# The output product of the last two token groups as seven products of quarters, chained in two PSUM banks

## The chip, the cores and the metric

The kernel runs on one core of a Trainium2 chip. The metric is the device time of one execution in microseconds, as the median of several executions. Before the change it is 307.48 us (three runs, 306.88 to 308.18).

## The reference

Attention over pooled keys and values, followed by a feed-forward layer whose activation is h - tanh(h):

```python
# q, k, v: [8 batches, 8 heads, 576, 64] fp32; pool = 8, Sp = 72
k_p = k.reshape(B, H, Sp, pool, D).mean(axis=3)
v_p = v.reshape(B, H, Sp, pool, D).mean(axis=3)
scores = scale * np.matmul(q, k_p.transpose(0, 1, 3, 2))
attn = softmax(scores)                       # written out in the reference
x = (attn @ v_p) with heads side by side     # [4608 tokens, 512]
h = x @ w_in                                 # w_in  [512, 2048]
g = h - np.tanh(h)
out = g @ w_out                              # w_out [2048, 512], out fp32
```

## The kernel before

The 4608 tokens are worked off in nine groups of 512. Groups 0 to 7 are the first 512 tokens of a batch each; a token 4p + j of the batch is row p of token block j. Group 8 gathers the 64 tokens left over from each of the eight batches; its token block tb holds the rest of batches 2tb and 2tb + 1, 64 rows each.

A group has two matmul stages on TensorE, both in bf16 with fp32 sums in PSUM. The first (`h_mms`, line 386) makes h transposed, in 16 units of 128 of the 2048 hidden features: four matmuls of 512 columns each into one PSUM bank. After every second unit `h_act` lets ScalarE (ACT) take the tanh of two banks into `t_sb` (line 399) and VectorE (DVE) subtract it, which gives two of the 16 slices of `gT` in bf16 (line 400). `gT` is [128 features of a slice, 16 slices, 512 tokens]. The second stage (`o_mms`, line 429) multiplies `gT` with `w2b` ([128, 16 slices, 512 output features], bf16): for each of the four token blocks 16 matmuls of 128 tokens by 512 columns are summed in one bank, so 64 matmuls a group. The list `UNITS` orders them by (token block, quarter of the slices), so that the last slices are asked for late. `o_store` (line 450) copies a finished bank into one of four rotating tiles `o_sb`, and SyncE's queue (SP) stores it: one DMA of 128 rows for groups 0 to 7, two of 64 rows each for group 8. For the very last token block `o_last` splits the columns in 384 and 128, each with its own copy and two stores, one from SP and one from ACT (line 464).

While group g runs, the attention of batch g + 1 is made in between, by the dictionary `plan`: step kinds "s" (scores, lines 275, 287, 290), "e" (exponential, line 303), "t" and "x" (transposes by DMA on SP), "a" (values and normalising, lines 339, 360, 361), at fixed places among the units. Pooling of k and v runs on GpSimd (POOL, lines 193 to 220); loads of q, k and v are issued from SP by `load_for`. Group 6 makes the attention of batch 7 and of the last left-over tokens; groups 7 and 8 hold the two matmul stages alone. The raw tiles `k_raw`, `v_raw` and `q_raw` (two each, fp32, by parity of the batch) are read for the last time in groups 4 and 5 (even batches), and in groups 5 and 6 (batch 7). Each engine works through its own instructions in the order in which the program gives them, since the schedule is manual; TensorE, ACT, DVE, POOL and SP wait for each other only on the data and the buffers.

PSUM has eight banks of 512 fp32 columns. The h units of a group take banks 0 to 5 in turn (`i % 6`); the output product of groups 1 to 8 takes banks 4 and 5 by the parity of the token block, and `o_last` banks 0 and 1.

Of the kernel before, what the change touches and what calls it, by code (L numbers as in the profile page):

```python
# [8 lines left out]
FP32 = mybir.dt.float32  # L9
# [11 lines left out]
R = 4  # L21
# [5 lines left out]
NG = 9  # L27
NT = 5
NK = H * G
KP = 2 * G  # L30
D1 = D + 1
SCALE = 1.0 / (POOL * float(D) ** 0.5)


@with_exitstack
def kernel(
# [13 lines left out]
    const = ctx.enter_context(tc.tile_pool(name="const", bufs=1))  # L50
    work = ctx.enter_context(tc.tile_pool(name="work", bufs=2))
    tpool = ctx.enter_context(tc.tile_pool(name="tpool", bufs=3))
    opool = ctx.enter_context(tc.tile_pool(name="opool", bufs=4))
    psum = ctx.enter_context(tc.tile_pool(name="psum", bufs=1, space=PSUM))
    PS = psum.tile([128, 8, 512], FP32, name="PS")
    ctx.enter_context(tc.manual_schedule())
# [4 lines left out]
    def two(banks, n):  # L61
# [32 lines left out]
    v_sm = const.tile([128, NT, 1, D], FP32, name="v_sm")  # L94
    x_tl = const.tile([128, 1, 2, 4, D], BF16, name="x_tl")
    warm = const.tile([128, 1], FP32, name="warm")
    v_bf = [
        v_raw[i]
        .rearrange("p t n -> p (t n)")
# [1 line left out]
        .rearrange("p (t n) -> p t n", t=NT)  # L101
        for i in range(2)
    ]

    def xT_of(g):
        return xTs[g % 2] if g < B else xTt
# [320 lines left out]
    def o_mms(tb, i0, i1, bank, c0=0, c1=DM):  # L427
        for i in range(i0, i1):
            nc.tensor.matmul(  # L429
                PS[:, bank, 0 : c1 - c0],  # L430
                lhsT=gT[:, i, tb * 128 : (tb + 1) * 128],
                rhs=w2b[:, i, c0:c1],
                start=(i == 0),
                stop=(i == NHID - 1),
            )

    def out_rows(g, tb):
        if g < B:
            blk = out[g * S : g * S + QA, :].rearrange("(p j) m -> p j m", j=R)
            return [(0, 128, blk[:, tb, :])]  # L440
        return [
            (64 * s, 64 * s + 64, out[(2 * tb + s) * S + QA : (2 * tb + s + 1) * S, :])
            for s in range(2)
        ]
# [1 line left out]
    stores = []  # L446

    def o_store(g, tb, bank, eng):
        o_sb = opool.tile([128, DM], FP32, name="o_sb", tag="o_sb")
        eng(out=o_sb[:, :], in_=PS[:, bank, :])  # L450
        for r0, r1, dst in out_rows(g, tb):
            stores.append(
                lambda dst=dst, src=o_sb[r0:r1, :]: nc.sync.dma_start(out=dst, in_=src)
            )

    def o_last(g, tb, banks):
        o_sb = opool.tile([128, DM], FP32, name="o_sb", tag="o_sb")
        for n, (c0, c1, eng) in enumerate(
            ((0, 384, nc.scalar.copy), (384, DM, nc.vector.tensor_copy))
        ):  # L460
            o_mms(tb, 0, NHID, banks[n], c0, c1)
            eng(out=o_sb[:, c0:c1], in_=PS[:, banks[n], 0 : c1 - c0])
            for s, (r0, r1, dst) in enumerate(out_rows(g, tb)):
                (nc.sync, nc.scalar)[s].dma_start(out=dst[:, c0:c1], in_=o_sb[r0:r1, c0:c1])

    def fill(n, bank, cols=512):
        for _ in range(n):
# [234 lines left out]
    PAIRS = ((6, 7), (0, 1), (2, 3))  # L702
    UNITS = [(0, 0), (0, 1), (0, 2), (1, 0), (1, 1), (0, 3), (1, 2), (1, 3)]
    UNITS += [(tb, qd) for tb in (2, 3) for qd in range(4)]
    hn = [0]
    for g in range(1, NG):
        nb = g + 1 if g + 1 < B else None
        more = nb is not None and nb + 1 < B

        tail = {2: 0, 3: 1, 5: 2, 7: 3}.get(nb)  # L710
        plan = {}
        if nb is not None:
            units = [(s_block(nb, j), av_block(nb), slot(4 * nb + j)) for j in range(4)]
            s_pairs, a_pairs = [0, 0, 0, 1, 2], [0, 1, 0, 2, 1]
            plan = {
                -12: [("s", 0)],
                -9: [("e", 0)],
                -8: [("s", 1)],
                -5: [("e", 1), ("t", 0)],
                -3: [("s", 2)],  # L720
                0: [("e", 2)],
                1: [("s", 3)],
                3: [("e", 3), ("t", 1)],
                4: [("a", 0)],
                5: [("a", 1), ("x", 0)],
                9: [("a", 2), ("a", 3), ("x", 1)],
            }
            if g == 1:
                plan[-10], plan[-7], plan[-5] = plan.pop(-12), plan.pop(-9), plan.pop(-8)
                plan[-2], plan[-1] = [("e", 1), ("t", 0)], plan.pop(-3)  # L730
            if tail is not None:
                units.append((s_tail(tail), av_tail(tail), slot_tl))
                plan[3].append(("s", 4))
                plan[4] += [("e", 4), ("t", 2)]
                if g == 1:
                    plan[6], plan[7] = plan[4][:1], plan.pop(5)
                    plan[4] = plan[4][1:]
                    plan[10] = plan.pop(9)
                plan[12] = [("a", 4), ("x", 2)]
            xs = [x_pair(), x_pair(), x_tl]  # L740
        if nb is not None:
            pool_v(nb, nc.gpsimd)
        shs = {}

        def step(kind, n):
            if kind == "t":
                e_turn_dma(units[2 * n][2], 0, 2 if n < 2 else 1)
                if tail and n == 0:
                    turn_tail(tail)
                return  # L750
            if kind == "x":
                x_turn_dma(xs[n], *((nb, 2 * n, 2) if n < 2 else (B, tail, 1)))
                return
            s, a, sl = units[n]
            if kind == "s":
                bk = PAIRS[s_pairs[n]]
                s_mms(s, bk)
                shs[n] = s_shift(bk)
            elif kind == "e":
                s_exp(shs[n], sl)  # L760
            else:
                bk = PAIRS[a_pairs[n]]
                av_mms(sl, a, bk)
                normalise(bk, xs[n // 2][:, n % 2, :, :, :])

        for i in range(NHID):
            h_mms(g, i, i % 6)
            if i % 2:
                h_act(i - 1, (i - 1) % 6)
            for it in plan.get(i - NHID, ()):  # L770
                step(*it)
            if more and i in (13, 15):
                q_cast(nb + 1, se, i - 13, i - 11)
        for u, (tb, qd) in enumerate(UNITS):
            if g == NG - 1 and tb == 3:
                o_last(g, tb, (0, 1))
                break
            o_mms(tb, qd * 4, qd * 4 + 4, 4 + tb % 2)
            if qd == 3:
                o_store(g, tb, 4 + tb % 2, se)  # L780
                run(stores)
            for it in plan.get(u, ()):
                step(*it)
            if u == 0 and more:
                pool_k(nb + 1, nc.gpsimd)
            if more:
                if u == 0:
                    q_turn_dma(nb + 1)
                    run(stores)
                if u == 4:  # L790
                    k_turn_dma(nb + 1)
                    k_place_kT(nb + 1, ge)
                if u == 11 and nb % 2 == 0:
                    run(tail_pieces(nb // 2))
                    tail_cast(nb // 2)
            if u == 13:
                load_for(g + 1)

# [1 line left out]
_INS = ['q', 'k', 'v', 'moe_w_in', 'moe_w_out']  # L800
# [26 lines left out]
```

## Time and profile before

| | |
|---|---|
| median of 3 runs | 307.48 us (306.88 to 308.18) |
| the profiled execution's own time | 306.89 us |
| its span, first to last instruction | 305.10 us |
| mean granted TensorE clock | 0.994 |
| TensorE matmul / weight load busy | 290.4 / 150.4 us |
| DVE / ACT / POOL busy | 179.4 / 142.3 / 113.5 us |
| group 7: first stage, output product | 246.16 to 259.97, 259.97 to 273.79 us |
| group 8: first stage, output product | 273.79 to 287.60, 287.60 to 301.63 us |

In the rows shown below a line has the source line, the engine, the operation, what is written and read, the shapes, and how often it occurs; behind the bar stand the busy time in us and the mean of one in ns, and behind the next bar the idle time of the engine before it and what ended it. In a timeline the first number is the start in us from the span's start and the second is how long the run of instructions takes. Matmul ends are modelled and overlap the next start, so lengths of matmul work are taken from start to start. PEld is the weight load of TensorE; SPq and ACTq are the issuing of DMAs by those engines. The row PEclk gives the granted clock in tenths, for 40 slices of the span.

### The profile page before, as it was taken

The numbers are of one execution on the slowest core, as the hardware profiler recorded it, in microseconds if no ns is written. First come the engines' busy times: TensorE is split into PE (matmuls) and PEld (weight loads), VectorE is DVE, ScalarE is ACT, GpSimd is POOL, SyncE is SP. The second block draws the span as 40 slices with busy tenths as digits, with TensorE's granted clock in tenths as the row PEclk, the third lists the DMA queues.
The fourth block names the chain that finished last, engine by engine and source line by source line (L and its number), as shares of the span: only waits on it lengthen the run. The fifth ranks groups of instructions, "written<-read, shape, count | busy, mean of one in ns | idle before, by whom it ended". The sixth has DMA issues, their size and how long they took to land.

```text
span 305.1 us, 4524 instructions
## 1 busy us (share of the span) xinstructions
PE 290.4 (95%) x1734; PEld 150.4 (49%) x1757; DVE 179.4 (59%) x250; ACT 142.3 (47%) x186; POOL 113.5 (37%) x101
## 2 busy tenths in 40 slices
PE   5779989899999999999999999999999999999995
PEld 1457955444554455445544554455445544444443
DVE  4696766458844993398249933983399336305700
ACT  2467756157504751476147613761474136225511
POOL 7544929209610791097109710971080000000000
PEclk9799999999999999999999999999999999999999
DMA  7999997898999998876898799879803830020023
GB/s 232 220 223 309 217 281 164 157 269 288 198 219 213 345 161 183 284 261 123 200 275 280 142 165 282 289 91 219 252 15 73 183 94 0 9 97 34 0 63 77
DMA packets 85894, 54.84 MB, mean 180 GB/s; under 512 B 60368, under 2 KB 73040, under 8 KB 85872
## 3 DMA queue, kind: packets, MB, share of 16 engines
q1 hardware_dynamic: 78192, 44.84, 58.7%
q0 software_dynamic: 6400, 8.91, 14.2%
q10 hardware_dynamic: 1280, 0.79, 0.9%
q8 instruction: 14, 0.23, 0.3%
q14 instruction: 8, 0.07, 0.1%
HBM read 36.70 MB, written 9.44 MB: 151 GB/s over the span
## 4 chain that ended last, share of the span: by engine, by line
PE 84%; DVE 5%; DMA 4%; ACT 4%; issue 1%; ACTq 0%; DVEq 0%
PE PS L429 38%; PE PS L386 35%; PE PS L339 4%; PE PS L275 3%; PE PS L408 2%; DMA k_raw<-in_k_dram 2%; DMA xT<-x_sb 2%; PE PS L256 1%; ACT E L303 1%; DVE sh L290 1%; DVE mx L287 1%; DVE gT L421 1%; DVE x_sb L361 1%; ACT qT L521 1%; ACT t_sb L420 1%
## 5 line engine op out<-in xcount | busy, mean ns | idle before, releaser
L429 PE MATMUL PS<-w2b,gT 128*128 128x512 bf16 (+2 forms) x570 | 131.4, 373 | 1.4 <-ACT v_sm L651 0.2
L400 DVE TENSOR_TENSOR gT<-PS,t_sb 128x1024 bf16<-128x1024 f32 x64 | 77.2, 1220 | 63.4 <-ACT t_sb L399 63.4
L386 PE MATMUL PS<-xT,w1b 128*128 128x512 bf16 x448 | 100.6, 379 | 1.1 <-DMA xT<-x_sb 1.1
L399 ACT ACTIVATE t_sb<-PS 128x1024 f32<-128x1024 f32 x64 | 65.6, 1024 | 44.5 <-PE PS L386 44.5
L429 PEld LDWEIGHTS <-gT 128*128 128x128 bf16 x592 | 54.8, 98 | 58.5 <-issue 0.5
L386 PEld LDWEIGHTS <-w1b 128*128 128x128 bf16 x512 | 49.3, 98 | 58.0 <-issue 2.3
L450 ACT COPY o_sb<-PS 128x512 f32<-128x512 f32 x33 | 19.3, 584 | 73.6 <-PE PS L429 73.6
L208 POOL TENSOR_TENSOR v_raw<-v_raw 128x1280 f32<-128x1280 f32 x6 | 17.4, 2906 | 40.7 <-DMA v_raw<-in_v_dram 40.7
L303 ACT ACTIVATE E<-sh 128x576 bf16<-128x576 f32 x32 | 21.8, 681 | 19.8 <-DVE sh L290 19.8
L287 DVE TENSOR_REDUCE mx<-PS 128x8 f32<-128x576 f32 x36 | 26.9, 748 | 5.6 <-PE PS L275 5.6
L290 DVE TENSOR_TENSOR sh<-PS,mx 128x576 f32<-128x576 f32 x36 | 27.3, 757 | 1.2
L360 DVE RECIPROCAL rden<-PS 128x8 f32<-128x8 f32 x36 | 7.3, 204 | 27.5 <-PE PS L339 27.4
L361 DVE TENSOR_TENSOR x_sb<-PS,rden 128x512 bf16<-128x512 f32 x32 | 22.1, 691 | 1.1
L193 POOL TENSOR_TENSOR k_raw<-k_raw 128x1280 f32<-128x1280 f32 x7 | 20.3, 2905 | 0.1
L244 ACT CAST q_bf<-q_raw 128x1024 bf16<-128x1024 f32 x14 | 14.4, 1038 | 5.5 <-DMA q_raw<-in_q_dram 5.5
L339 PEld LDWEIGHTS <-ET 128*128 128x128 bf16 x192 | 13.1, 98 | 6.1 <-ACT ET L322 0.8
L230 POOL COPY KB<-kT 64x288 bf16<-64x288 bf16 x12 | 5.1, 421 | 29.5 <-DMA kT<-kd 17.8
L408 PE MATMUL PS<-xT,w1b 128*128 128x256 bf16 x128 | 15.3, 273 | 0.7 <-ACT xT L378 0.7
L339 PE MATMUL PS<-VB,ET 128*128 128x130 bf16 (+2 forms) x192 | 15.7, 221 | 0.2 <-ACT ET L322 0.2
L275 PE MATMUL PS<-KB,qT 128*128 128x144 bf16 x128 | 13.1, 226 | 1.3 <-ACT KB L230 0.9
L275 PEld LDWEIGHTS <-qT 128*128 128x128 bf16 x128 | 9.9, 98 | 8.8 <-issue 1.6
L386 PE MATMUL PS<-xTt,w1b 128*128 128x512 bf16 x64 | 14.0, 379 | 0.0
(75 smaller groups left out, 171.7 us busy)
## 6 DMA issues: line engine op xcount, KB each, us to landing
out_dram<-o_sb SPq DMA_DIRECT2D x32, 256.0 KB, 2.7
k_raw<-in_k_dram SPq DMA_DIRECT2D x14, 512.0 KB, 8.4
v_raw<-in_v_dram SPq DMA_DIRECT2D x12, 512.0 KB, 5.0
q_raw<-in_q_dram SPq DMA_DIRECT2D x11, 512.0 KB, 6.8
w1b<-in_moe_w_in_dram POOLq DMA_DIRECT2D x4, 512.0 KB, 9.0
q_raw<-in_q_dram POOLq DMA_DIRECT2D x2, 1024.0 KB, 15.1
w2b<-in_moe_w_out_dram POOLq DMA_DIRECT2D x4, 512.0 KB, 19.2
v_raw<-in_v_dram POOLq DMA_DIRECT2D x2, 512.0 KB, 13.7
```

The costliest lines, as they stand in the source:

```text
L193: eng.tensor_tensor(out=r[:, :, 0:4, :], in0=r[:, :, 0:4, :], in1=r[:, :, 4:8, :], op=ALU.add)
L275: nc.tensor.matmul(PS[ps, banks[m // 2], KP * (m % 2) : KP * (m % 2) + KP], lhsT=qT[:, m, :], rhs=KB[kb][:, m, :], start=True, stop=True,)
L287: nc.vector.reduce_max(out=mx.rearrange("p k h o -> p k (h o)"), in_=sc, axis=AX.X)
L290: nc.vector.tensor_tensor(out=sh[:, :, :, :], in0=sc, in1=mx.to_broadcast([128, 2, 4, G]), op=ALU.subtract)
L303: nc.scalar.activation(out=E[:, e, :, :].rearrange("p t c -> p (t c)")[:, 0:NK], in_=sh.rearrange("p k h c -> p (k h c)"), func=ACT.Exp, s ...
L339: nc.tensor.matmul(PS[ps, banks[half], D1 * h : D1 * (h + s1 - s0)], lhsT=ET[:, t, c0 : c0 + (ps.stop - ps.start)], rhs=VB[kb][:, t, s0:s1 ...
L361: nc.vector.tensor_tensor(out=x_sb, in0=ps[:, :, :, 0:D], in1=rden.to_broadcast([128, 2, 4, D]), op=ALU.mult,)
L386: nc.tensor.matmul(PS[:, bank, :].rearrange("p (j c) -> p j c", j=R), lhsT=w1b[:, fb, i * 128 : (i + 1) * 128], rhs=xT_of(g)[:, :, fb, :], ...
L399: nc.scalar.activation(out=t_sb[:, :, :], in_=ps, func=ACT.Tanh)
L400: nc.vector.tensor_sub(out=gT[:, i : i + 2, :], in0=ps, in1=t_sb[:, :, :])
L408: h_mm_last[0] = nc.tensor.matmul(PS[:, bank, 256 * s : 256 * s + 256].rearrange("p (j c) -> p j c", j=2), lhsT=w1b[:, fb, (2 * n + s) * 1 ...
L429: nc.tensor.matmul(PS[:, bank, 0 : c1 - c0], lhsT=gT[:, i, tb * 128 : (tb + 1) * 128], rhs=w2b[:, i, c0:c1], start=(i == 0), stop=(i == NH ...
```

## The change

For groups 7 and 8 the output product is written with halves of three sizes. The 512 tokens are cut in C1 (blocks 0, 1) and C2 (blocks 2, 3), the 16 slices in LO (0 to 7) and HI (8 to 15), and the 512 output features in C1 and C2. Eight quarter products would be the ordinary way; seven products of sums of quarters (Winograd's form of Strassen's algorithm) give the same result. Each is two token blocks times eight slices, 16 matmuls of 256 columns, 112 a group.

- Four sums of quarters of `w2b` (T1 to T4) are made once, as eight DVE operations of 128x1024 in bf16, one behind each of the units 8 to 15 of group 6's output product. They lie in the raw tiles of k and v of the even batches.
- Four sums of quarters of `gT` (S1 to S4) are made in each of the two groups, as eight DVE operations of 128x1024: the first half of S3 behind the subtraction of units 10, 11, the first half of S2 behind that of units 12, 13, the other six behind the last. They lie in the raw tiles of q.
- The products come in the order 4, 2, 7, 1, 6, 5, 3. Product 2 has bank 2. All others are summed one on top of the other in bank 0 (first token block) and bank 1 (second), without clearing after product 4; ACT copies out the states after 4 and 7 (`n0`, `n1`), and the results are differences to those states, taken by DVE (products 1, 5, 3) or a plain copy by ACT (product 6). The next product may write a bank only when that copy or difference is done.
- The quarter of product 1 lacks product 2 (`p2`), which POOL adds in SBUF (`finish_11`, one operation of 128x512 fp32).
- The h units of groups 7 and 8 take the bank pairs (2, 3), (4, 5), (0, 1) in turn.
- The results lie in two tiles `o_hs`, one for each half of the tokens, which the other groups use too, in place of the four rotating `o_sb`. Group 7 stores a half with one DMA of all its columns. Group 8 stores each quarter on its own, as four DMAs of 64 rows and 256 columns: behind the POOL addition, behind products 6 and 5, all from SP, and behind product 3, two from SP and two from ACT. `o_last` goes.

```diff
--- before.py
+++ after.py
@@ -29,6 +29,9 @@
 NK = H * G
 KP = 2 * G
 D1 = D + 1
+NQ = NHID // 2
+HC = DM // 2
+SEVEN = (7, 8)
 SCALE = 1.0 / (POOL * float(D) ** 0.5)
 
 
@@ -50,7 +53,6 @@
     const = ctx.enter_context(tc.tile_pool(name="const", bufs=1))
     work = ctx.enter_context(tc.tile_pool(name="work", bufs=2))
     tpool = ctx.enter_context(tc.tile_pool(name="tpool", bufs=3))
-    opool = ctx.enter_context(tc.tile_pool(name="opool", bufs=4))
     psum = ctx.enter_context(tc.tile_pool(name="psum", bufs=1, space=PSUM))
     PS = psum.tile([128, 8, 512], FP32, name="PS")
     ctx.enter_context(tc.manual_schedule())
@@ -94,6 +96,7 @@
     v_sm = const.tile([128, NT, 1, D], FP32, name="v_sm")
     x_tl = const.tile([128, 1, 2, 4, D], BF16, name="x_tl")
     warm = const.tile([128, 1], FP32, name="warm")
+    o_hs = [const.tile([128, 2, DM], FP32, name=f"o_h{i}") for i in range(2)]
     v_bf = [
         v_raw[i]
         .rearrange("p t n -> p (t n)")
@@ -101,6 +104,19 @@
         .rearrange("p (t n) -> p t n", t=NT)
         for i in range(2)
     ]
+
+
+    def quarters(raw):
+        return [
+            raw[:, n * NQ * HC : (n + 1) * NQ * HC].rearrange("p (i c) -> p i c", c=HC)
+            for n in range(2)
+        ]
+
+    T1, T2 = quarters(k_raw[0].rearrange("p t n -> p (t n)").bitcast(BF16))
+    T3, T4 = quarters(v_raw[0].rearrange("p t n -> p (t n)").bitcast(BF16))
+    S1, S2 = quarters(q_raw[0].rearrange("p h j d -> p (h j d)").bitcast(BF16))
+    S3, S4 = quarters(q_raw[1].rearrange("p h j d -> p (h j d)").bitcast(BF16))
+    p2, n0, n1 = [k_raw[1][:, n, :].rearrange("p (b c) -> p b c", b=2) for n in range(3)]
 
     def xT_of(g):
         return xTs[g % 2] if g < B else xTt
@@ -446,22 +462,102 @@
     stores = []
 
     def o_store(g, tb, bank, eng):
-        o_sb = opool.tile([128, DM], FP32, name="o_sb", tag="o_sb")
+        o_sb = o_hs[tb // 2][:, tb % 2, :]
         eng(out=o_sb[:, :], in_=PS[:, bank, :])
         for r0, r1, dst in out_rows(g, tb):
             stores.append(
                 lambda dst=dst, src=o_sb[r0:r1, :]: nc.sync.dma_start(out=dst, in_=src)
             )
 
-    def o_last(g, tb, banks):
-        o_sb = opool.tile([128, DM], FP32, name="o_sb", tag="o_sb")
-        for n, (c0, c1, eng) in enumerate(
-            ((0, 384, nc.scalar.copy), (384, DM, nc.vector.tensor_copy))
-        ):
-            o_mms(tb, 0, NHID, banks[n], c0, c1)
-            eng(out=o_sb[:, c0:c1], in_=PS[:, banks[n], 0 : c1 - c0])
-            for s, (r0, r1, dst) in enumerate(out_rows(g, tb)):
-                (nc.sync, nc.scalar)[s].dma_start(out=dst[:, c0:c1], in_=o_sb[r0:r1, c0:c1])
+
+
+    LO, HI = slice(0, NQ), slice(NQ, NHID)
+    C1, C2 = slice(0, HC), slice(HC, DM)
+
+    def w_sums():
+        b11, b12, b21, b22 = ((HI, C1), (HI, C2), (LO, C1), (LO, C2))
+        w = lambda q: w2b[:, q[0], q[1]]
+        ops = [
+            (T1, w(b12), w(b11)),
+            (T2, w(b22), T1),
+            (T3, w(b22), w(b12)),
+            (T4, w(b21), T2),
+        ]
+        return [
+            lambda o=o, x=x, y=y, n=n: nc.vector.tensor_sub(
+                out=o[:, n : n + 4, :], in0=x[:, n : n + 4, :], in1=y[:, n : n + 4, :]
+            )
+            for n in (0, 4)
+            for o, x, y in ops
+        ]
+
+    def g_sum(n, i0, i1):
+        i = slice(i0, i1)
+        a11, a12 = gT[:, NQ + i0 : NQ + i1, C1], gT[:, i, C1]
+        a21, a22 = gT[:, NQ + i0 : NQ + i1, C2], gT[:, i, C2]
+        o, x, y, op = {
+            1: (S1, a21, a22, ALU.add),
+            2: (S2, a22, S3[:, i, :], ALU.subtract),
+            3: (S3, a11, a21, ALU.subtract),
+            4: (S4, a12, S2[:, i, :], ALU.subtract),
+        }[n]
+        return nc.vector.tensor_tensor(out=o[:, i, :], in0=x, in1=y, op=op)
+
+    XB, YB = 2, (0, 1)
+    PRODUCTS = ("4", "2", "7", "1", "6", "5", "3")
+
+    def product(n, b):
+
+        A, a0, B_ = {
+            "1": (gT[:, HI, C1], 0, w2b[:, HI, C1]),
+            "2": (gT[:, LO, C1], 0, w2b[:, LO, C1]),
+            "3": (S4, 0, w2b[:, LO, C2]),
+            "4": (gT[:, LO, C2], 0, T4),
+            "5": (S1, 0, T1),
+            "6": (S2, 0, T2),
+            "7": (S3, 0, T3),
+        }[n]
+        ps = PS[:, XB, HC * b : HC * b + HC] if n == "2" else PS[:, YB[b], 0:HC]
+        for i in range(NQ):
+            nc.tensor.matmul(
+                ps,
+                lhsT=A[:, i, 128 * b : 128 * b + 128],
+                rhs=B_[:, i, :],
+                start=(n in "24" and i == 0),
+                stop=(i == NQ - 1),
+                skip_group_check=True,
+            )
+
+    def evacuate(n, b):
+        ps = PS[:, YB[b], 0:HC]
+        if n == "2":
+            if b == 1:
+                nc.scalar.copy(out=p2, in_=PS[:, XB, :].rearrange("p (b c) -> p b c", b=2))
+        elif n in "47":
+            nc.scalar.copy(out={"4": n0, "7": n1}[n][:, b, :], in_=ps)
+        elif n == "6":
+            nc.scalar.copy(out=o_hs[1][:, b, C1], in_=ps)
+        else:
+            dst, sub = {
+                "1": (o_hs[0][:, b, C1], n1),
+                "5": (o_hs[1][:, b, C2], n0),
+                "3": (o_hs[0][:, b, C2], n1),
+            }[n]
+            nc.vector.tensor_sub(out=dst, in0=ps, in1=sub[:, b, :])
+
+    def finish_11(eng):
+        o = o_hs[0][:, :, C1]
+        eng.tensor_tensor(out=o, in0=o, in1=p2, op=ALU.add)
+
+    def store_half(g, hf, cols=slice(0, DM), engs=(nc.sync, nc.sync)):
+        o = o_hs[hf]
+        if g < B:
+            blk = out[g * S : g * S + QA, :].rearrange("(p j) m -> p j m", j=R)
+            nc.sync.dma_start(out=blk[:, 2 * hf : 2 * hf + 2, cols], in_=o[:, :, cols])
+            return
+        for b in range(2):
+            for s, (r0, r1, dst) in enumerate(out_rows(g, 2 * hf + b)):
+                engs[s].dma_start(out=dst[:, cols], in_=o[r0:r1, b, cols])
 
     def fill(n, bank, cols=512):
         for _ in range(n):
@@ -702,7 +798,9 @@
     PAIRS = ((6, 7), (0, 1), (2, 3))
     UNITS = [(0, 0), (0, 1), (0, 2), (1, 0), (1, 1), (0, 3), (1, 2), (1, 3)]
     UNITS += [(tb, qd) for tb in (2, 3) for qd in range(4)]
-    hn = [0]
+    HB = ((2, 3), (4, 5), (0, 1))
+    w_ops = w_sums()
+    LATE = [(3, 4), (2, 4), (1, 0), (1, 4), (4, 0), (4, 4)]
     for g in range(1, NG):
         nb = g + 1 if g + 1 < B else None
         more = nb is not None and nb + 1 < B
@@ -764,17 +862,34 @@
                 normalise(bk, xs[n // 2][:, n % 2, :, :, :])
 
         for i in range(NHID):
-            h_mms(g, i, i % 6)
+            bk = HB[i // 2 % 3][i % 2] if g in SEVEN else i % 6
+            h_mms(g, i, bk)
             if i % 2:
-                h_act(i - 1, (i - 1) % 6)
+                h_act(i - 1, bk - 1)
+                if g in SEVEN:
+                    for n, i0 in {11: [(3, 0)], 13: [(2, 0)], 15: LATE}.get(i, ()):
+                        g_sum(n, i0, i0 + 4)
             for it in plan.get(i - NHID, ()):
                 step(*it)
             if more and i in (13, 15):
                 q_cast(nb + 1, se, i - 13, i - 11)
-        for u, (tb, qd) in enumerate(UNITS):
-            if g == NG - 1 and tb == 3:
-                o_last(g, tb, (0, 1))
-                break
+        for u in range(14 if g in SEVEN else 0):
+            n, b = PRODUCTS[u // 2], u % 2
+            product(n, b)
+            evacuate(n, b)
+            if b == 0:
+                continue
+            if n == "1":
+                finish_11(nc.gpsimd)
+                if g == NG - 1:
+                    store_half(g, 0, C1)
+            elif g == NG - 1 and n in "65":
+                store_half(g, 1, C1 if n == "6" else C2)
+            elif g == NG - 1 and n == "3":
+                store_half(g, 0, C2, (nc.sync, nc.scalar))
+            elif n in "53":
+                store_half(g, 0 if n == "3" else 1)
+        for u, (tb, qd) in enumerate(() if g in SEVEN else UNITS):
             o_mms(tb, qd * 4, qd * 4 + 4, 4 + tb % 2)
             if qd == 3:
                 o_store(g, tb, 4 + tb % 2, se)
@@ -795,6 +910,8 @@
                     tail_cast(nb // 2)
             if u == 13:
                 load_for(g + 1)
+            if g == SEVEN[0] - 1 and u >= 8 and w_ops:
+                w_ops.pop(0)()
 
 # ---- launch: one core; inputs and outputs as the reference has them ----
 _INS = ['q', 'k', 'v', 'moe_w_in', 'moe_w_out']
```

## The prediction

> **What bounds the kernel now.** I read the page first: busy times, slices and the chain that ended last.
>
> ```profile
> PE 290.4 (95%) x1734; PEld 150.4 (49%) x1757; DVE 179.4 (59%) x250; ACT 142.3 (47%) x186; POOL 113.5 (37%) x101
> ...
> PEclk9799999999999999999999999999999999999999
> ...
> PE 84%; DVE 5%; DMA 4%; ACT 4%; issue 1%; ACTq 0%; DVEq 0%
> ```
>
> TensorE is busy for 95% of the span at nearly full granted clock, and 84% of the chain is matmuls. So the order of matmuls sets the time; what is saved there is a gain until another wait takes its place. Next I read the timeline of TensorE over the stages that the change rewrites, and one stretch of 256-column matmuls in group 0:
>
> ```profile
> 28.09 8.02 PE L408 MATMUL PS<-xT,w1b 128*128 128x256 bf16 x72
> ...
> 246.16 13.98 PE L386 MATMUL PS<-xT,w1b 128*128 128x512 bf16 x64
> 259.97 13.98 PE L429 MATMUL PS<-w2b,gT 128*128 128x512 bf16 x62
> 273.79 13.98 PE L386 MATMUL PS<-xTt,w1b 128*128 128x512 bf16 x64
> 287.60 14.02 PE L429 MATMUL PS<-w2b,gT 128*128 128x512 bf16 x79
> ```
>
> Groups 7 and 8 run without a gap. An output product (line 429) takes 273.79 - 259.97 = 13.82 us: 64 matmuls of 512 columns at 215.9 ns (two records are missing). The 72 matmuls of 256 columns, each with its own weight load, run from 28.09 to the next group's start at 35.95: 109.2 ns each. Then the grouped rows, shapes apart, for what the new work may cost:
>
> ```profile
> L400 DVE TENSOR_TENSOR gT<-PS,t_sb 128x1024 bf16<-128x1024 f32 x64 | 77.2, 1220 | 63.4 <-ACT t_sb L399 63.4
> L193 DVE TENSOR_TENSOR k_raw<-k_raw 128x512 f32<-128x512 f32 x2 | 1.4, 688 | 1.3 <-DMA k_raw<-in_k_dram 1.3
> L193 DVE TENSOR_TENSOR k_raw<-k_raw 128x256 f32<-128x256 f32 x1 | 0.4, 425 | 2.0 <-DMA k_raw<-in_k_dram 2.0
> L462 ACT COPY o_sb<-PS 128x384 f32<-128x384 f32 x1 | 0.5, 479 | 2.0 <-PE PS L429 2.0
> L450 ACT COPY o_sb<-PS 128x512 f32<-128x512 f32 x33 | 19.3, 584 | 73.6 <-PE PS L429 73.6
> L211 POOL TENSOR_TENSOR v_raw<-v_raw 128x640 f32<-128x640 f32 x6 | 9.3, 1542 | 0.5
> L214 POOL TENSOR_TENSOR v_raw<-v_raw 128x320 f32<-128x320 f32 x6 | 5.2, 865 | 0.5
> ```
>
> Last, the end: SP's timeline and the source row of the closing stores.
>
> ```profile
> 295.32 1.10 SPq L453 DMA_DIRECT2D out_dram<-o_sb  x2
> ...
> 301.26 1.18 SPq L464 DMA_DIRECT2D out_dram<-o_sb  x2
> ...
> L464 SPq DMA_DIRECT2D out_dram<-o_sb x2: 467/467/467, 301.3 to 302.0; - x2
> ...
> 301.65 0.29 DVE L462 COPY o_sb<-PS 128x128 f32<-128x128 f32 x1 [11.57 <-PE PS L429]
> ```
>
> The last matmul ends at 301.63, a copy of 0.29 us follows, SP's last issue starts at 301.26 + 1.18 - 0.467 = 301.97, and the span ends at 305.10: 3.13 us after that start. An issue occupies SP for about half a microsecond, one after another; hidden now, that matters below.
>
> **The change part by part.** Times below count from the start of the group's output product (287.60 in group 8 of before); "first" and "second" are a product's two token blocks of 8 matmuls.
>
> *Matmuls.* 64 x 215.9 ns become 112 x 109.2 ns = 12.23 us: a gain of 1.59 us per group if nothing stalls. Here the Trainium skill ("TensorE: Matmul & The Clock Gate", Back-to-back issue gap) speaks against the change: pairs of weight load and matmul sustain about 131 ns at 512 columns and 81 ns at 128, by interpolation an estimated 98 ns at 256. By it the products would rise from 8.4 to 10.9 us a group; the trace disagrees with both lengths, and the rows stand.
>
> *Sums of gT.* Eight Vector operations a group, each 128x1024 in bf16, SBUF only. No row shows such a form. Bounds: 1.22 us (line 400, as many elements, but reading fp32 from PSUM) and 0.69 us (line 193, SBUF only, as many bytes per operand). I take 0.69, the row without PSUM and with equal bytes, and keep 1.22 for a rival. The Trainium skill ("VectorE: DVE Perf Modes", the perf-mode tier table) lists bf16 tensor_tensor in SBUF at twice the fp32 rate, which gives the same; no row of before shows it. In the trace an independent DVE operation starts 0.08 us before its predecessor's recorded end (220.77 after 219.63 + 1.22), a dependent one 0.03 after. The subtraction of units 10, 11 ends at -0.97, then: first S3 half to -0.25, subtraction of 12, 13 to 0.90, first S2 half to 1.51, subtraction of 14, 15 to 2.66 (2.49 before), and the six late halves end at 3.38, 4.10, 4.71, 5.32, 5.93 and 6.54. Product 7 needs the second half of S3 at 3.93: in time.
>
> *The chain in banks 0 and 1.* A matmul block's result reaches ACT or DVE 0.31 us after its last matmul starts (273 ns of row L408's mean + 0.04), and TensorE restarts 0.06 us after a release (DVE's sh ends at 74.80, the matmul starts at 74.86). A copy of 128x256 on ACT is 479 - 105 = 0.374 us by the step from 512 to 384 columns, on DVE 0.425 (line 193). Between the last matmul's start and the bank's next use lie 0.109 + 0.874 = 0.98 us; the hand-over takes 0.31 + 0.374 + 0.06 = 0.74 (ACT) or 0.80 (DVE). So products 1, 5 and 3 don't wait. Product 6 waits for the subtraction that empties product 1, and that stands on DVE's queue behind the six sums: from 6.46 to 6.89, matmul possible at 6.95, wanted at 6.99. Covered by 0.04 us, so costed at nothing; each 0.1 us more on a sum would uncover about 0.8 us.
>
> *Sums of w2b.* Eight operations on DVE in group 6. From the ninth unit of group 6's output product on DVE is nearly idle: from 237.2 to 249.19 it has 2.7 us of normalising. One fits before 240.07, three end at about 243.9 and push the tail's normalise by 0.2 us (its result is used in group 8, 30 us later), four end at 247.6, before the first subtraction at 249.19. Nothing, with 1.6 us of cover.
>
> *ACT and buffers.* Copies of 0.586 us (four, or three and a split) become one of 0.586 and six of 0.374 per group, in ACT's idle time after the last tanh. The ring of four o_sb tiles becomes four fixed slots, each reused after a whole group (some 28 us), with stores landing in 2.7 us. The banks of units 0 to 5 in group 7 (2, 3, then 4, 5, then 0, 1) are free: bank 5, the latest, is emptied at 246.95 and wanted at about 248.7. Nothing for all three.
>
> *The end.* Group 7's two stores are large but far from the end. In group 8 SP issues 4 + 4 + 4 + 2 = 14 stores where it issued 8; ACT keeps 2. The first four wait for the POOL addition: product 1's second block empties by 7.61, POOL takes about 1.27 us for 128x512 (between 865 ns for 320 elements and 1542 for 640), so SP starts at 8.95. The others queue behind: 13 issues of 0.467 to 0.59 us (L464, L453) with gaps of 0.04 make 0.51 to 0.60 each (the pair at 295.32 has 0.55). I take 0.54, nearest to that pair: the last issue starts at 8.95 + 7.02 = 15.97. Not backlogged, it would start at 12.9, once product 3's second block is subtracted (last matmul 12.12 + 0.31 + 0.43). In before it starts at 301.97 - 287.60 = 14.37. So group 8 ends 1.60 us later than before, plus 0.05 for a last store of 64 KB (96 KB landed in 2.1 us, 32 KB in 1.9). The product's gain in group 8 is lost whole.
>
> **Sum.** Group 7: -1.59. Group 8: +1.65. Rest: 0. The profiled execution took 306.89 us for a span of 305.10; it becomes 306.95. The median of before, 307.48, lies 0.59 above that execution, so I expect 307.5. With issue bounds of 0.51 and 0.60 the sum is -0.3 to +0.8, and bank hand-overs as long as the 512-column rows (0.59, 0.69) would add up to 0.6 in group 7: 307.1 to 308.9 for this case.
>
> **Rivals.**
> *The sums hold the bank (slower).* Place: DVE before the subtraction of product 1. At 1.22 us each, the second S3 half ends at 4.97 (product 7 stalls 1.1), the sixth late one at 10.78, product 6 starts at 11.19, and the product takes 16.43 us: +2.6 in group 7. Group 6's sums run to 250.9 and stall group 7 by 0.85. In group 8 the POOL addition ends at 12.8, the last issue starts near 19.8: +5.45. Sum +8.9: 316.4 us. It decides (over 0.5%) from about 0.82 us a sum: 0.84 in group 7 plus 0.5 at the start of SP's queue at 0.80. For it: line 400 is the only row with as many elements. Against: it reads PSUM in fp32.
>
> *SP's queue does not hold the end (faster).* The shortest store issue on line 453 is 0.33 us. At 0.33 + 0.05 the last issue starts at 13.9: -0.48 in group 8, -2.07 in all, 305.4 us; with no backlog at all -1.47 and -1.59, 304.4. For it: that row's minimum. Against: its median is 0.53, and the pairs in group 8 itself take 1.10 for two.
>
> **How the numbers follow.** Half a percent, 1.5 us, is about what a measurement of this kernel can tell from no change. My case has 0.68: 0.62 of it within that bound, 0.05 slower (stalls of bank and queue together), 0.01 faster. The slow sums have 0.18, all slower. The free queue has 0.14, 0.13 of it faster. So faster 0.14, same 0.63, slower 0.23. The range runs from 305.3 (the queue at its shortest issue) to 309.8 (sums of about 0.85 us); it leaves out some 0.06 below and 0.12 above. The likeliest case alone spans 307.1 to 308.9.
>
> **What would show it.** The new product line shows 112 matmuls in about 12.2 us in groups 7 and 8, and group 8's first matmul starts 1.6 us earlier, near 272.2. The DVE rows of the gT and w2b sums show about 0.69 us; 1.2 means the first rival. TensorE's idle time before product 6 is near nothing. On SP, 14 stores follow each other without a pause from about 9 us after the product's start, and the last starts 3 to 4 us after the last matmul, not at once. I am wrong if the stores' issues are well under 0.5 us, if the sums exceed 0.8, or if the POOL addition, whose row is an interpolation, ends much off 8.9: every microsecond there moves the end by one.

## The result and the profile after

The changed kernel takes 308.93 us (median of 8 runs, 308.49 to 309.52) against 307.36 us for the kernel before in the same comparison (8 runs): a ratio of 1.0046, 95% interval 1.0033 to 1.0060. It is slower by about 1.4 us, inside the half percent that I called no change (the interval's upper end, 1.0060, lies just beyond it). Its profiled execution took 308.93 us for a span of 307.2.

TensorE's timeline of the changed kernel from group 7 on (start in us, length, engine and line, operation, how many):

```profile
246.73 13.98 PE L402 MATMUL PS<-xT,w1b 128*128 128x512 bf16 x64
260.54 1.91 PE L522 MATMUL PS<-v_raw,gT 128*128 128x256 bf16 x16
...
271.02 1.91 PE L522 MATMUL PS<-w2b,q_raw 128*128 128x256 bf16 x16
272.77 13.98 PE L402 MATMUL PS<-xTt,w1b 128*128 128x512 bf16 x64
286.58 1.91 PE L522 MATMUL PS<-v_raw,gT 128*128 128x256 bf16 x16
...
291.82 1.91 PE L522 MATMUL PS<-w2b,gT 128*128 128x256 bf16 x16
293.90 3.65 PE L522 MATMUL PS<-k_raw,q_raw 128*128 128x256 bf16 x32 [0.16 <-DVE o_h L546]
297.39 1.91 PE L522 MATMUL PS<-w2b,q_raw 128*128 128x256 bf16 x16
```

Group 7's output product takes 272.77 - 260.54 = 12.23 us instead of 13.82, without a gap. In group 8 products 6 and 5 (they share one row) begin 0.33 us late: 293.90 - 286.58 = 7.32 instead of 64 x 0.1092 = 6.99.

The end of the changed kernel, first POOL's timeline:

```profile
294.35 1.27 POOL L550 TENSOR_TENSOR o_h<-o_h,k_raw 128x512 f32<-128x512 f32 x1 [24.78 <-DVE o_h L546]
```

SP's timeline, with the last of its issues:

```profile
295.64 8.87 SPq L560 DMA_DIRECT2D out_dram<-o_h  x14
...
303.97 0.55 SPq L560 DMA_DIRECT2D out_dram<-o_h  x1
```

The source row of the closing stores (shortest, median and longest issue in ns, first and last start):

```profile
L560 SPq DMA_DIRECT2D out_dram<-o_h x14: 546/555/588, 295.6 to 304.0; - x14
```

And two stretches of the table of busy times (length, then PE, PEld, DVE, ACT and POOL with their instructions, granted clock, DMA share, GB/s):

```profile
301.00:302.00 1.00, 0.00 (x0) 0.00 (x0) 0.00 (x0) 0.00 (x0) 0.00 (x0) 0.81 0.56 137
302.00:303.00 1.00, 0.00 (x0) 0.00 (x0) 0.00 (x0) 0.00 (x0) 0.00 (x0) 0.50 0.53 131
```

From POOL's end at 295.62 to 304.52 SP does nothing but issue 14 stores, one after another. The last subtraction ends at 299.75, yet the last store is issued only at 303.97; in between no computing engine works, and in the two stretches shown the DMA engines are about half busy. So it is probably the issuing that is short here, and not the transfers; the kernels with fewer issues below test that. (The granted clock falls to 0.50 in these stretches, where no matmul is left.)

Where the 2.1 us between the two spans come from: group 7 starts 0.57 us later (246.73 against 246.16), in work that the change does not touch; over the eleven profiles behind this document that start lies between 245.94 and 248.48. From group 7's output product to group 8's it is 26.04 us instead of 27.63: -1.59. From there to the end it is 20.62 instead of 17.50: +3.12.

### The profile page after: what moved, and what is told of

It reads as the page before. It is cut to its first block, busy times and chain, and to the rows that moved or that the text cites. A ratio compares the mean times of both kernels' runs of the same rounds, so it can differ in the third digit from the quotient of the medians.

```text
span 307.2 us, 4773 instructions
## 1 busy us (share of the span) xinstructions
PE 288.9 (94%) x1837; PEld 159.5 (52%) x1837; DVE 198.9 (65%) x285; ACT 143.2 (47%) x192; POOL 116.2 (38%) x103
## 4 chain that ended last, share of the span: by engine, by line
PE 79%; DVE 8%; DMA 4%; ACT 4%; issue 1%; ACTq 0%; DVEq 0%
PE PS L402 34%; PE PS L445 28%; PE PS L522 6%; PE PS L355 4%; PE PS L291 3%; DMA k_raw<-in_k_dram 2%; PE PS L424 2%; DVE q_raw L504 2%; DVE gT L416 2%; PE PS L272 1%; DVE mx L303 1%; DVE sh L306 1%; DMA xT<-x_sb 1%; ACT E L319 1%; PE PS L564 1%
## 5 line engine op out<-in xcount | busy, mean ns | idle before, releaser
L445 PE MATMUL PS<-w2b,gT 128*128 128x512 bf16 x448 | 104.7, 379 | 0.2 <-ACT v_sm L747 0.2
L445 PEld LDWEIGHTS <-gT 128*128 128x128 bf16 x448 | 41.2, 98 | 44.0 <-issue 0.5
L466 ACT COPY o_h<-PS 128x512 f32<-128x512 f32 x26 | 15.2, 583 | 54.6 <-PE PS L445 54.6
L550 POOL TENSOR_TENSOR o_h<-o_h,k_raw 128x512 f32<-128x512 f32 x2 | 2.5, 1270 | 61.7 <-DVE o_h L546 61.7
L355 PEld LDWEIGHTS <-ET 128*128 128x128 bf16 x192 | 13.1, 98 | 6.3 <-ACT ET L338 0.8
```

The lines of the kernel that those rows point to most:

```text
L355: nc.tensor.matmul(PS[ps, banks[half], D1 * h : D1 * (h + s1 - s0)], lhsT=ET[:, t, c0 : c0 + (ps.stop - ps.start)], rhs=VB[kb][:, t, s0:s1 ...
L445: nc.tensor.matmul(PS[:, bank, 0 : c1 - c0], lhsT=gT[:, i, tb * 128 : (tb + 1) * 128], rhs=w2b[:, i, c0:c1], start=(i == 0), stop=(i == NH ...
```

## The experiments

The last two columns below are what tells the kernels apart; they leave out the scatter of the first 246 us. Lengths are from one profile each, ratios from the timed runs against the kernel before.

| kernel | ratio (95% interval) | group 7's to group 8's output product, us | from there to the end, us |
|---|---|---|---|
| before | 1 | 27.63 | 17.50 |
| changed | 1.0046 (1.0033 to 1.0060) | 26.04 | 20.62 |
| group 7 only | 0.9943 (0.9922 to 0.9964) | 26.04 | 17.64 |
| ten issues | 0.9956 (0.9935 to 0.9978) | 26.03 | 17.90 |
| merged stores | 0.9928 (0.9901 to 0.9954) | 26.04 | 17.30 |
| merged, again | 0.9949 (0.9931 to 0.9966) | 26.04 | 17.27 |
| merged, S4 later | 0.9958 (0.9941 to 0.9975) | 26.04 | 18.00 |
| merged, two more sums | 0.9999 (0.9984 to 1.0014) | 27.12 | 18.09 |
| merged, own result tiles | 0.9946 (0.9926 to 0.9967) | 26.04 | 17.30 |
| DVE adds, last stores split | 0.9900 (0.9884 to 0.9916) | 26.04 | 16.47 |
| the same, S4 later | 0.9898 (0.9882 to 0.9914) | 26.04 | 16.28 |

My theory was that the matmul gain is real in both groups, and that SP's issues at the end take group 8's share of it and more. The rivals: that the chained banks and sums eat the gain, or that the end is set by DVE, POOL or the transfers rather than by the number of issues.

### One part alone: group 7 only

```diff
-SEVEN = (7, 8)
+SEVEN = (7,)
```

with `o_last` back in group 8, on the fixed result tiles.

> Group 7 in seven products, group 8's output product, its stores and o_last as before the change. Theory (the matmul gain is real and is lost only in group 8's stores): group 7's product takes 12.23 us instead of 13.82, group 8 ends 17.5 us after its output product starts, so 1.6 us faster than before, ratio 0.995. Rival 1 (something else in the change costs time in every part, since group 7 began 0.57 us later in the profile of the changed kernel): 1.0 us faster, ratio 0.997. Rival 2 (the chained banks and sums cost what the matmuls gain): no difference, ratio 1.000.

Measured: 305.94 us, ratio 0.9943. Its second stage in group 8 and its stores are those of before, and take 17.64 us to the end where before took 17.50. The product alone gains what the matmul count says, and rival 2 falls; rival 1, at 0.997, lies outside the interval. So all the loss of the whole change sits in group 8.

### Fewer issues, the same bytes: ten on SP

```diff
-            elif g == NG - 1 and n in "65":
-                store_half(g, 1, C1 if n == "6" else C2)
+            elif g == NG - 1 and n == "5":
+                store_half(g, 1)
...
-            elif n in "53":
+            elif g < NG - 1 and n in "53":
```

> The changed kernel, but in group 8 the half C2 of the tokens is stored behind product 5 with whole rows of 512 columns: four stores instead of eight, SP issues 10 instead of 14. Theory (SP's issues, 0.64 us each in a row, set the end): four from 9.06, four until 14.2, the last starts at about 14.8 us instead of 17.39 after the product's start: 2.6 us less than the changed kernel, 306.3 us, ratio to before 0.9965. Rival (the end is set by TensorE, DVE or POOL, not by the number of stores): as the changed kernel, ratio 1.0046.

Measured: 306.03 us, ratio 0.9956 (0.9965 expected). SP's timeline of this kernel, whose output product in group 8 starts at 286.40:

```profile
295.46 6.33 SPq L560 DMA_DIRECT2D out_dram<-o_h  x10
...
300.60 1.19 SPq L560 DMA_DIRECT2D out_dram<-o_h  x2
```

The tenth issue ends at 301.79 and starts at 301.2, 14.8 us after the product's start, as forecast. Four issues fewer, 2.6 us earlier; the bytes are the same.

### Half the issues: two blocks in one store

```diff
-        for b in range(2):
-            for s, (r0, r1, dst) in enumerate(out_rows(g, 2 * hf + b)):
-                engs[s].dma_start(out=dst[:, cols], in_=o[r0:r1, b, cols])
+        rows = out.rearrange("(n r) m -> r n m", r=S)
+        for s in range(2):
+            n0_ = 4 * hf + s
+            engs[s].dma_start(
+                out=rows[QA:S, n0_ : n0_ + 3 : 2, cols], in_=o[64 * s : 64 * s + 64, :, cols]
+            )
```

> The changed kernel, but in group 8 a quarter's two token blocks go in one store for each 64 partitions: two stores of 128 rows of 1 KB for a quarter instead of four of 64 rows, SP issues 7 instead of 14, the rows and bytes stay. Theory (an issue costs the same whatever it moves): no queue is left at the end, the last store starts at about 12.9 us instead of 17.39: 4.5 us less than the changed kernel, 304.4 us, ratio to before 0.990. Rival (what costs is the number of rows: an issue of twice the rows takes 1.2 us): seven issues from 9.06 on end where about twelve did, last start at 16.3, 1.1 us less than the changed kernel, ratio 1.001. Rival (not the stores): ratio 1.0046.

Measured: 305.54 us, ratio 0.9928; in a second comparison 305.88 us, 0.9949.

> The kernel with merged stores once more, beside the three that follow, which are built from it. As in its first run: ratio to before 0.993, the last store starts 13.2 us after the product's start and the span ends 4.1 us after that.

The source row of the stores in the first profile:

```profile
L561 SPq DMA_DIRECT2D out_dram<-o_h x7: 595/597/685, 294.9 to 299.0; - x7
```

SP's last issue in its timeline:

```profile
299.00 0.60 SPq L561 DMA_DIRECT2D out_dram<-o_h  x1
```

Two stretches of its table of busy times:

```profile
298.00:299.00 1.00, 0.51 (x5) 0.21 (x3) 0.53 (x2) 0.00 (x0) 0.00 (x0) 1.00 0.83 198
299.00:300.00 1.00, 0.00 (x0) 0.00 (x0) 0.00 (x0) 0.00 (x0) 0.00 (x0) 1.00 0.85 200
```

An issue of 128 rows takes 0.597 us (median) where one of 64 took 0.555: nearly all of the cost is the issue, not the rows, and that rival falls. The last issue starts at 299.00 - 285.80 = 13.2 us, close to the 12.9 expected, straight behind the last subtraction (it ends at 298.97) and just as close behind the issue before it: the queue has no slack yet, but it no longer adds to the end. But the end comes only 20.62 - 17.30 = 3.3 us earlier, not 4.5: the span now ends 4.1 us after that issue instead of 3.2. The DMA engines are 0.83 to 0.85 busy at 200 GB/s in the last stretches, and the last stores are 128 KB each and land in 2.4 to 2.8 us instead of 2.0 to 2.3. The longer landing goes with the size and not with the busy engines: the first of SP's stores, for which the engines are free, lands in 2.5 us just as SP's last one does. The last to land is ACT's store, 2.8 us after its issue starts at 299.01, and from there to the end it is 1.3 us, about as in the changed kernel (303.97 + 2.0 to 307.2: 1.2). A kernel with smaller last stores follows below.

### S4 behind the bank's release

The kernels from here on start from merged stores, and their edits are shown against that kernel.

```diff
-    LATE = [(3, 4), (2, 4), (1, 0), (1, 4), (4, 0), (4, 4)]
+    LATE = [(3, 4), (2, 4), (1, 0), (1, 4)]
...
                 finish_11(nc.gpsimd)
+                for i0 in (0, 4):
+                    g_sum(4, i0, i0 + 4)
```

> Merged stores, and the two late halves of S4 stand on DVE's queue behind the subtractions that empty product 1 instead of ahead of them; S4 is wanted by product 3 alone, 10.5 us after the product's start, and would be ready at about 9. Theory: the 0.16 us in which TensorE waited before product 6 in group 8 go, nothing else changes: 0.1 to 0.2 us less than with merged stores alone, ratio 0.990. Rival (DVE's later subtractions are pushed and a later product waits): 0.2 to 0.5 us more.

Measured: 306.44 us, 0.9958, no better than merged stores (0.9928 and 0.9949), and 0.7 us longer at the end. The theory fell. DVE's timeline of group 8 shows why:

```profile
294.33 0.42 DVE L546 TENSOR_TENSOR o_h<-PS,k_raw 128x256 f32<-128x256 f32 x1 [0.72 <-PE PS L522]
294.67 2.36 DVE L504 TENSOR_TENSOR q_raw<-gT,q_raw 128x1024 bf16<-128x1024 bf16 x2
```

And POOL's:

```profile
294.83 1.65 POOL L550 TENSOR_TENSOR o_h<-o_h,k_raw 128x512 f32<-128x512 f32 x1 [24.78 <-DVE o_h L546]
```

S4's two sums took 1.28 us elsewhere and take 2.36 here; the POOL addition that now runs at the same time takes 1.65 us instead of 1.27. SP starts 9.80 us after the product's start instead of 9.05. Of these 0.75 us the longer addition makes 0.38; the other 0.37 come before it, since the second subtraction, and with it POOL, starts that much later (an idle time on DVE, to which the last experiment comes back). Each of the two reads two operands in SBUF. In the changed kernel the two never ran at once, because the sums stood ahead of the subtraction that POOL waits for.

### How much cover the sums have: two more of them

```diff
-    LATE = [(3, 4), (2, 4), (1, 0), (1, 4), (4, 0), (4, 4)]
+    LATE = [(3, 4), (2, 4), (1, 0), (1, 4), (4, 0), (4, 4), (4, 0), (4, 4)]
```

> Merged stores, with the two late halves of S4 made twice: 2 x 0.61 us more on DVE ahead of the subtraction that empties product 1. Theory (that subtraction has no cover): product 6 waits about 1.2 us longer in group 7 and in group 8, and both count at the end: 2.4 us more than merged stores alone, ratio 1.001. Rival (there is cover, or the closing stores hide it in group 8): 0 to 1.2 us more, ratio 0.993 to 0.997.

Measured: 307.51 us, 0.9999. Product 6 of group 7 now waits, as this kernel's timeline of TensorE shows:

```profile
266.03 1.91 PE L522 MATMUL PS<-w2b,gT 128*128 128x256 bf16 x16
268.86 3.65 PE L522 MATMUL PS<-k_raw,q_raw 128*128 128x256 bf16 x32 [0.93 <-DVE o_h L546]
```

It starts 268.86 - 260.79 = 8.07 us after its group's product instead of 6.99: 1.08 us for 1.2 us of sums. In group 8 it starts 0.77 us later than with merged stores (8.08 against 7.31): there the subtraction now starts at once behind the sums, so that the idle time on DVE of the last experiment is not added to them. Together 1.85 us, where I expected 2.4; the ratio rises by 0.005 to 0.007 (1.5 to 2.2 us). The subtraction that empties product 1 has about 0.1 us of cover (slack) in group 7.

### Smaller last stores, and the addition on DVE

```diff
+        if engs is None:
+            for b in range(2):
+                for s, (r0, r1, dst) in enumerate(out_rows(g, 2 * hf + b)):
+                    (nc.sync, nc.scalar)[s].dma_start(out=dst[:, cols], in_=o[r0:r1, b, cols])
+            return
...
-                finish_11(nc.gpsimd)
+                finish_11(nc.vector)
...
-                store_half(g, 1, C1 if n == "6" else C2)
+                store_half(
+                    g, 1, C1 if n == "6" else C2, (nc.sync, nc.sync if n == "6" else nc.scalar)
+                )
...
-                store_half(g, 0, C2, (nc.sync, nc.scalar))
+                store_half(g, 0, C2, None)
```

> Merged stores, but the addition of p2 on DVE instead of POOL, product 5's second store from ACT, and product 3's quarter in four stores of 64 KB again, so that the first block's leave before the last subtraction. Theory (with merged stores the end is set by 256 KB that the DMA engines get at once at the end, at 0.8 to 0.85 of their time busy): SP starts at 8.4 instead of 9.05, the last issue still at 13.2, but the span ends 3.2 us after it instead of 4.1: 0.9 us less than merged stores, ratio 0.990. Rival (a fixed closing time, or DVE's addition delays a bank): as merged stores or up to 0.5 us slower, ratio 0.993 to 0.995.

Measured: 304.54 us, ratio 0.9900, as forecast. SP's last two issues, whose group starts its product at 285.93:

```profile
294.37 3.50 SPq L566 DMA_DIRECT2D out_dram<-o_h  x5
298.14 1.36 SPq L561 DMA_DIRECT2D out_dram<-o_h  x2
```

The queue has a gap before the last two, and another between them: it is no longer what ends last. The last one starts at 299.02, 13.1 us in, as with merged stores, and the span ends 3.4 us later instead of 4.1. Three things were changed at once here (the adding engine, one store moved to ACT, the size of the last stores); the nearly unchanged start of the last issue says that the 0.7 us belong to what is still to land then, and ACT's last store, now of 64 KB, lands in 2.2 us instead of 2.8; but the runs don't part the three. More of the issues on ACT's queue, with nothing else changed, was not tried.

The next edit is made to this kernel:

```diff
                 finish_11(nc.vector)
+                for i0 in (0, 4):
+                    g_sum(4, i0, i0 + 4)
```

> As the kernel before it, with the late halves of S4 behind the addition of p2 on DVE. Theory (moving S4 cost time earlier because S4's sums and POOL's addition ran at once and slowed each other, 2.36 us for two sums instead of 1.28 and 1.65 for the addition instead of 1.27): without POOL the two sums take 1.28 us again, product 6 has no wait of 0.3 us in group 8, 0.2 us less than the kernel before, ratio 0.989. Rival (S4's place itself costs, whoever adds): two sums at 1.28 all the same, and 0.3 us or more slower than the kernel before, ratio 0.991 or above; or two sums still at 2.4, and POOL had no part in it.

Measured: 304.40 us, 0.9898; this and 0.9900 can't be told apart in time, but the profiles can. DVE's timeline of group 8:

```profile
294.44 0.69 DVE L550 TENSOR_TENSOR o_h<-o_h,k_raw 128x512 f32<-128x512 f32 x1
295.05 1.28 DVE L504 TENSOR_TENSOR q_raw<-gT,q_raw 128x1024 bf16<-128x1024 bf16 x2
```

The chain that ended last, in order of time:

```profile
286.89 12.24 PE PS L522 x112
299.13 0.02 issue
299.15 0.42 DVE o_h L546
```

Without POOL beside them the two sums take 1.28 us again, and the same place for S4 now costs nothing: here the chain shows all 112 matmuls of group 8 in one piece of 12.24 us, so the idle time on DVE is gone as well. The overlap with POOL was what lengthened the sums; the loss that S4's move brought before is not shown to come from it alone. The Trainium skill says the same of the pair ("SBUF — State Buffer", Who interferes with whom): a Vector instruction with two SBUF inputs contends with a GpSimd instruction that reads SBUF, since its second input uses a read interface that the two share. The runs agree, with 2.36 us for two sums against 1.28. This kernel, with the seven products in both groups, is about 1% (3.1 us) faster than the kernel before.

### What stays open: 0.4 us on DVE in group 8

In the changed kernel the chain of group 8 shows a gap between the sums and the subtraction that empties product 1:

```profile
289.97 2.96 DVE q_raw L504 x5
292.92 0.05 issue
292.97 0.05 DVEq L546
293.02 0.40 issue
293.42 0.44 DVE o_h L546
```

The chain leaves the five sums (the second S2 half, S1, S4) at 292.93; by its own row the last one ends at 293.07. The product's first block has been ready since its last matmul's start at 292.58 plus 0.31, 292.89. Yet the subtraction starts at 293.42, behind an instruction of DVE's queue and 0.40 us that the profile puts on nothing; for 0.35 of them DVE is idle. In group 7 it starts at once. I tried result tiles of their own for group 8:

```diff
+    o_h8 = [v_raw[1][:, 2 * i : 2 * i + 2, :] for i in range(2)]
...
+        if g == NG - 1:
+            cur[0] = o_h8
```

> Merged stores, but group 8's results lie in tiles of their own (the raw tile of v of batch 7), so that its subtractions don't also have to wait for group 7's stores and POOL addition on the same tile. Theory (the 0.4 us on DVE before the subtraction that empties product 1 in group 8, which the profile puts on nothing, comes with that additional wait, which stands on DVE's queue as an instruction of its own; in group 7 that subtraction starts at once): the subtraction starts within 0.1 us of the last sum, product 6 starts 7.0 us after group 8's product instead of 7.3, 0.3 us less than merged stores alone, ratio 0.992 to 0.994. Rival (the gap has another cause, such as fetching instructions late in the program): product 6 starts at 7.3 as before.

Measured: 305.73 us, 0.9946, as merged stores, and the gap is the same (product 6 starts 293.91 - 286.60 = 7.31 us in). So it isn't the wait for group 7's stores. That tile has older readers on POOL, so a wait of some kind may remain. With S4 moved and no POOL it is gone (12.24 us in one piece), with S4 moved and POOL it appears one subtraction later, with the addition on DVE it is 0.24 us, and with two more sums ahead it doesn't show. For the rival, late fetching of instructions, the trace gives no support: in the changed kernel instructions are transferred at 291.34, for 0.42 us, and at 294.12, and no transfer at all is in flight from 292.9 to 293.45. The cause is not settled. The gap costs 0.3 us in the changed kernel and is half of SP's late start with S4 moved; the account of the closing stores doesn't rest on it.

## Why the prediction was right and where it was off

The range (305.3 to 309.8) holds 308.93, and no change within half a percent came true, and so did the mechanism: group 7 gains, group 8 loses it to SP's queue. "Group 7 only" and the kernels with fewer issues show each half. The middle was off: I expected a sum of +0.06 us, and it is about +1.5 (-1.59 and +3.12). 308.93 lies at the end of what I gave for my own case (307.1 to 308.9), and a bound of 1.5 us was met with 1.4: that it still counts as no change is partly luck. Step by step:

- *Matmuls.* 12.23 us predicted for 112, 12.23 measured in group 7. The pitch (start to start) of 109.2 ns from group 0 carried over: the matmuls got shorter in sum, not longer. So the trace doesn't bear out what the prediction cites of the Trainium skill ("TensorE: Matmul & The Clock Gate", Back-to-back issue gap), 131 ns sustained at 512 columns and an estimated 98 at 256: the rows before and after the change give 215.9 and 109.2.
- *Sums of gT.* 0.69 us taken from the row with equal bytes, 0.68 to 0.69 measured. The rival at 1.22 us is out. The Trainium skill ("VectorE: DVE Perf Modes", the perf-mode tier table), with twice the fp32 rate for bf16, had the same; the trace agrees, as these rows of the changed kernel show:

```profile
259.61 0.69 DVE L504 TENSOR_TENSOR q_raw<-gT 128x1024 bf16<-128x1024 bf16 x1
...
264.54 1.28 DVE L504 TENSOR_TENSOR q_raw<-gT 128x1024 bf16<-128x1024 bf16 x2
...
267.03 0.42 DVE L546 TENSOR_TENSOR o_h<-PS,k_raw 128x256 f32<-128x256 f32 x1
```

- *The chain in banks 0 and 1.* Product 6 wanted its bank at 6.99, I had it free at 6.95; in group 7 the subtraction starts 6.49 in (267.03 - 260.54; 6.46 predicted) and no matmul waits. In group 8 it comes 0.33 us late by the gap that stays open. The slope of 0.8 us per 0.1 us on each sum can't be read from a run that adds two whole sums; that 1.2 us more of them cost 1.08 us in group 7 shows the lack of cover.
- *Sums of w2b, ACT copies, buffers.* Costed at nothing, and group 7's first stage runs without a gap. The last of these sums ends at 247.70, 2.06 us before DVE's next work.
- *POOL's addition.* 1.27 us interpolated, 1.27 measured; SP starts 9.06 us in (8.95 predicted).
- *The issues: the step that failed.* I priced one at 0.54 us with its gap, "nearest to that pair", from pairs of issues with pauses in between, and bounded it by 0.60. In an unbroken row of 14 an issue occupies SP for 0.546 to 0.588 us, and the next starts 0.05 or 0.09 us after its end: 0.64 each (8.33 us for 13), above my upper bound. That is 1.3 us over 13 issues; with 0.1 from POOL's start it gives the last issue at 17.39 us instead of 15.97, 4.7 us after the last matmul where I had 3 to 4. What follows it took 3.23 us (3.18 predicted). Part of this could have been read beforehand. My own terms, 0.59 us and a gap of 0.04, make 0.63 and not 0.60; with that bound the sum would have reached +1.2. And the kernel before also had a slower pair than the one I took:

```profile
293.59 1.20 SPq L453 DMA_DIRECT2D out_dram<-o_sb  x2
```

- *The free queue* (the fast rival) needed issues of 0.38 us, and no row of the runs came near. The mechanism that it named as the way to a gain was right: with the queue out of the way the change is worth 1% (in a kernel that also adds on DVE and splits its last stores).

## What to carry to other kernels

A gain in the last stage counts only as far as the closing stores can follow it: count the DMA issues on each queue from the moment the first result of the last stage is ready, price an unbroken row of them by its own pitch, and compare the sum with what is left of the computing. Cutting the output into more, earlier pieces lengthens the end as soon as the issues take longer than the computing behind which they hide; here a store that carries two blocks cost nearly the same issue as one that carries one (0.597 against 0.555 us). Smaller last stores came with an earlier end in the one kernel that had them, beside two other changes. And before an operation is moved "into idle time" on DVE, look at what POOL does in that time.

## What the runs showed of the hardware that I had not expected

- In an unbroken row, stores of 64 rows of 1 KB started 0.64 us apart on SP; with 128 rows a store occupies SP for 0.60 us instead of 0.555. In the kernel before, a store of 64 rows behind a pause occupied it for 0.467.
- With the issues halved, the DMA engines are 0.83 to 0.85 busy at about 200 GB/s in the last stretches, but that is not what holds the last stores: of 128 KB each, SP's land in 2.4 to 2.5 us whether the engines are free or busy, ACT's in 2.8; of 64 KB, in the changed kernel, in 2.0 to 2.3.
- Two bf16 sums of 128x1024 in SBUF on DVE took 2.36 us beside a POOL addition of 128x512 fp32, and that took 1.65 us; apart they take 1.28 and 1.27.
